# A three-stage kernel whose first batch of attention is done in two passes, with the first feed-forward in groups of 320 and 256 tokens

## Chip, cores and metric

One core of a Trainium2 chip runs the whole program. The metric is the device time of one execution in microseconds, the median of the runs, lower is better.

## The reference

Three stages follow one another, all in float32 (the weights come as float64 and are split by the kernel):

```python
# q, k, v: (4 batches, 8 heads, 576 tokens, 64)
scores = scale * np.matmul(q, k.transpose(0, 1, 3, 2))
mask = pos[:, None] // 64 >= pos[None, :] // 64        # blocks of 64 tokens, causal
attn = softmax(np.where(mask, scores, -1e9))
x = np.matmul(attn, v)                                 # to (2304 tokens, 512)
h = x @ moe_w_in                                       # 512 x 2048
x = np.maximum(0.01 * h, h) @ moe_w_out                # 2048 x 512
h = x @ moe2_w_in
P = a[0] + a[1] * h + a[2] * h**2 + a[3] * h**3
Q = 1.0 + abs(b[0]) * abs(h) + abs(b[1]) * h**2
out = (P / (Q + 1e-6)) @ moe2_w_out
```

## The kernel before

**Split products.** For accuracy most operands are split into a high and a low part (fp32r), and a product is summed from three matmuls: high by high, high by low, low by high. The first batch's attention is plain fp32, whose matmuls appear as two instructions each.

**Attention.** The 32 heads (4 batches of 8) are walked one after another in the loop over `heads`. A head has 576 queries in five tiles of 128 with `KEYS` = 64, 192, 320, 448 and 576 keys (`FIRST` gives each tile's first query). Each letter of the order string is one step of head n: `1` splits q and k of head n+1 (`a1`) and issues loads of q and k; `v` splits v (`a1v`) and, for odd heads, issues the load of a later pair's v (`load_v`); `x`, `y`, `z` compute scores of tile 4, tiles 3 and 2, tiles 1 and 0 (`a2_part`: matmuls L291 or L297, row maxima on VectorE L303, exponentials on ScalarE L309), after the last of them `a2_norm` (L315, L316, and five multiplications on GpSimd, L319); `a` and `b` transpose the probabilities of head n-1 on TensorE (L346) and copy them from PSUM (`evacuate`, L329 to L339); `4` multiplies those of head n-2 by the values (`a4`, L374, L378) and writes the result into the token tiles `X[b]` (L391 to L398). In the first batch (`n < NSF`, `WHOLE`), q is scaled on ScalarE by L245 and `pTw`, a view of `acc`, holds the transposed probabilities.

**First feed-forward.** `moe1(b)` is a generator over one batch of 576 tokens. It has 32 units: 16 of `in` (128 hidden columns each) and 16 of `out` (4 groups times 4 column tiles of the result). A unit is 12 products in two halves of 288 columns, so 24 matmuls (L455), summed in one PSUM tile and then read by ScalarE and VectorE (L468 to L477). `fill(n)` issues the next n matmuls; after each step of a head the numbers of `FILL` or `FILL1` are issued (93 a head). The feed-forward of a batch is queued when the last head of the batch has been applied; so none runs during the first batch's attention, and the fourth batch's runs after the attention. The high weights of it stay in SBUF (`w1i`, `w1o`); the low weights are loaded from DRAM (`W1L`) by `prep_w1`, two units ahead, into three buffers (L429).

**Conversion.** The float64 weights are read as pairs of integers in 64 blocks of 512 KB (`load_block`, L148), three staging buffers `cs`. `convert()` is a generator with two half-steps a block. ScalarE (L168; GpSimd for the first 16 blocks, L166) scales the high word, ScalarE the low word (L172); VectorE puts the sign into the low word (L179) and joins both words (L181); ScalarE rounds to the high part (L184), GpSimd subtracts to the low part (L185); SP writes the parts to DRAM (L156). `pace` issues half-steps so that by the end of head n there are `due[n]` of them; `prep_w1` forces more if a unit needs them (`cv_to`, by groups of four blocks, `NEED`). Blocks of 128 rows by 512 columns are converted group by group.

**Second feed-forward.** From about 683 us `moe2` streams all tokens in chunks of 512 through the second pair of weights (L558, L612).

**Queues and PSUM.** SP's order of DMA issues is the program's; the other engines' order is a scheduler's that follows the program's order closely. All tiles of PSUM in the attention and the first feed-forward share one pool of four (`psA`, 1024 columns each).

```python
due = [0, 2, 4, 5, 9, 11, 13, 17, 22, 29, 36, 42, 48, 59, 65] + [65 + 63 * n // 17 for n in range(1, 18)]
ORDER = "4vx1yabz"
ORDER0 = "1xy4azbv"
ORDERS = "1yzx4vab"
FILL = (12, 1, 0, 8, 18, 9, 13, 32)
ORDER1 = "14vxyabz"
FILL1 = (0, 10, 5, 7, 18, 10, 7, 36)
```

## Time and profile before

| | us |
|---|---|
| median of three runs | 1080.43 |
| the three runs | 1082.78, 1080.43, 1076.47 |
| profiled execution, its time | 1077.4 |
| its span, first to last instruction | 1075.6 |
| TensorE matmul busy | 1015.4 (94%) |
| VectorE busy | 770.2 (72%) |
| ScalarE busy | 661.4 (61%) |
| GpSimd busy | 314.2 (29%) |
| mean granted TensorE clock | 0.986 |

Busy time is the time in which an engine executes at least one instruction; matmuls are pipelined and their ends are modelled, so a busy TensorE isn't one at its peak. The page's second part gives the same in 40 slices of 26.9 us: TensorE's row is `6878888898999999999999999899999999999998`, in tenths. PE is TensorE's matmuls, PEld its weight loads, DVE VectorE, ACT ScalarE, POOL GpSimd, SP the queue that issues DMAs. Names such as L455 are lines of the kernel before.

### The profile page before, as it was taken

To read this page: it belongs to the slowest core of one execution; us is meant where nothing else is said; L and a number is where in the kernel's file an instruction comes from. 1 tells how busy PE (TensorE), PEld (TensorE's weight loads), DVE (VectorE), ACT (ScalarE), POOL (GpSimd) and SP (SyncE) were. 2 spreads that over 40 slices of the span, in tenths; PEclk is the share of its full clock that TensorE was granted. 3 is DMA by queue.
4 is the path that set the end of the run, shared out by engine and by line. 5 is a ranking of instruction groups with operands and counts; after the bars stand their busy time and mean duration, and the time that the engine had idled before them with its cause. 6 is when DMAs were issued, how large, how long until landed. Compare 5 with 4: busy or idle time off the path is not lost.

```text
span 1075.6 us, 16845 instructions
## 1 busy us (share of the span) xinstructions
PE 1015.4 (94%) x6120; PEld 911.1 (85%) x6120; DVE 770.2 (72%) x1261; ACT 661.4 (61%) x1319; POOL 314.2 (29%) x368
## 2 busy tenths in 40 slices
PE   6878888898999999999999999899999999999998
PEld 4557888898989999999999999788888888888887
DVE  3778778886767775877632222698988888888876
ACT  5766656855756665666632111777776676676675
POOL 5687545555444555545320001100000000000000
PEclk9999899999999999999999999999999999999999
DMA  7458566856766567665445845812000110110010
GB/s 190 135 150 252 155 192 189 261 169 203 218 190 175 185 201 237 200 196 168 145 132 197 329 127 171 340 56 79 4 36 9 70 40 1 40 40 1 1 40 20
DMA packets 99954, 149.01 MB, mean 139 GB/s; under 512 B 8224, under 2 KB 52256, under 8 KB 99872
## 3 DMA queue, kind: packets, MB, share of 16 engines
q1 hardware_dynamic: 99872, 147.95, 43.7%
q8 instruction: 48, 0.79, 0.3%
q14 instruction: 34, 0.28, 0.1%
HBM read 108.01 MB, written 39.32 MB: 137 GB/s over the span
## 4 chain that ended last, share of the span: by engine, by line
PE 53%; issue 11%; DMA 8%; DVE 6%; ACT 3%; POOL 2%; SPq 1%; POOLq 0%; ACTq 0%; DVEq 0%
PE o L612 18%; PE h L558 18%; PE M L455 12%; DMA cs<-in_moe_w_in_dram 4%; DMA cs<-in_moe_w_out_dram 3%; PE T L297 2%; PE T L346 2%; PE T L378 1%; POOL acc L482 1%; DVE cl L181 1%; ACT cs L168 1%; ACT cs L172 1%; DVE cs L179 1%; DVE pTl L339 1%; DVE nm L303 1%
## 5 line engine op out<-in xcount | busy, mean ns | idle before, releaser
L319 POOL TENSOR_SCALAR PB<-PB,sm 128x448 f32<-128x448 f32 (+4 forms) x160 | 104.7, 674 | 58.0 <-DVE sm L316 49.5
L309 ACT ACTIVATE PB<-T,nm 128x448 f32<-128x448 f32 (+4 forms) x160 | 83.1, 524 | 55.8 <-DVE nm L303 52.0
L455 PE MATMUL M<-gh,wl 128*128 128x288 f32 x512 | 114.0, 299 | 1.1 <-DMA wl<-w1l 1.1
L455 PE MATMUL M<-gh,w1o 128*128 128x288 f32 x512 | 113.8, 300 | 1.3 <-DVE pTl L339 0.6
L455 PE MATMUL M<-gl,w1o 128*128 128x288 f32 x512 | 111.6, 298 | 1.0 <-DVE gl L470 1.0
L570 ACT ACTIVATE ea<-h,coef 128x512 f32<-128x512 f32 (+1 forms) x80 | 51.7, 647 | 92.7 <-PE h L558 88.9
L470 DVE TENSOR_TENSOR gl<-M,gh 128x576 fp32r<-128x576 f32 x64 | 47.8, 749 | 65.7 <-ACT M L469 65.6
L558 PE MATMUL h<-x2h,w2h 128*128 128x512 f32 (+1 forms) x240 | 89.6, 373 | 4.1 <-DVE eu L581 3.2
L455 PE MATMUL M<-xh,w1i 128*128 128x288 f32 x512 | 84.6, 299 | 8.5 <-DVE pTl L339 3.8
L179 DVE SCALAR_TENSOR_TENSOR cs<-cs 128x512 int32<-128x512 int32 x64 | 60.1, 938 | 44.7 <-ACT cs L172 33.2
L558 PE MATMUL h<-x2h,w2l 128*128 128x512 f32 (+1 forms) x240 | 89.4, 373 | 0.0
L558 PE MATMUL h<-x2l,w2h 128*128 128x512 f32 (+1 forms) x240 | 89.3, 372 | 0.0
L455 PE MATMUL M<-xl,w1i 128*128 128x288 f32 x512 | 86.0, 301 | 2.2 <-DVE xl L392 1.3
L468 ACT ACTIVATE gh<-M 128x576 fp32r<-128x576 f32 x64 | 41.7, 652 | 75.3 <-PE M L455 75.0
L303 DVE TENSOR_REDUCE nm<-T 128x1 f32<-128x448 f32 (+4 forms) x160 | 71.5, 479 | 21.7 <-PE T L291 13.5
L573 DVE SCALAR_TENSOR_TENSOR ea<-eh,coef,ea 128x512 f32<-128x512 f32 (+1 forms) x80 | 55.9, 699 | 41.4 <-ACT eh L571 40.8
L455 PEld LDWEIGHTS M<-gh,wl 128*128 128x128 f32 x512 | 83.6, 190 | 1.6 <-DMA wl<-w1l 1.6
L455 PEld LDWEIGHTS M<-gh,w1o 128*128 128x128 f32 x512 | 83.0, 190 | 2.2 <-ACT w1i L184 0.8
L612 PE MATMUL o<-w2h,g2l 128*128 128x512 f32 x216 | 84.9, 393 | 0.0
L612 PE MATMUL o<-w2h,g2h 128*128 128x512 f32 x216 | 84.8, 393 | 0.0
L612 PE MATMUL o<-w2l,g2h 128*128 128x512 f32 x216 | 84.6, 392 | 0.0
L455 PEld LDWEIGHTS M<-gl,w1o 128*128 128x128 f32 x512 | 83.1, 190 | 1.3 <-DVE gl L470 1.3
(113 smaller groups left out, 2614.9 us busy)
## 6 DMA issues: line engine op xcount, KB each, us to landing
wl<-w1l SPq DMA_DIRECT2D x128, 256.0 KB, 3.0
cs<-in_moe_w_in_dram SPq DMA_DIRECT2D x32, 512.0 KB, 5.3
cs<-in_moe_w_out_dram SPq DMA_DIRECT2D x32, 512.0 KB, 4.6
w1l<-cl SPq DMA_DIRECT2D x32, 256.0 KB, 5.0
w2h<-ch SPq DMA_DIRECT2D x32, 256.0 KB, 4.9
w2l<-cl SPq DMA_DIRECT2D x32, 256.0 KB, 5.1
w2h<-w2h SPq DMA_DIRECT2D x12, 512.0 KB, 7.4
w2l<-w2l SPq DMA_DIRECT2D x12, 512.0 KB, 8.1
```

Of the source, the lines that this page charges most:

```text
L179: nc.vector.scalar_tensor_tensor(lo, hi, -(2 ** 31), lo, ALU.bitwise_and, ALU.bitwise_or)
L297: nc.tensor.matmul(T[:, po:po + w], lhsT=lhs[e][:, FIRST[i]:FIRST[i] + P], rhs=rhs[e][:, c:c + w], start=(lhs is QT), stop=(lhs is QM),)
L303: nc.vector.tensor_reduce(nm[:, i:i + 1], sc, axis=AX.X, op=ALU.max, negate=True)
L309: nc.scalar.activation(PB[e][i][:, 0:ln], sc, AF.Exp, scale=SCALE if n == 0 else 1.0, bias=nm[:, i:i + 1], accum_out=sm[:, i:i + 1])
L319: nc.gpsimd.tensor_scalar(PB[e][i][:, 0:ln], PB[e][i][:, 0:ln], sm[:, i:i + 1], 1.0, ALU.mult, ALU.mult)
L455: nc.tensor.matmul(T[:, e * 512:e * 512 + NH2], lhsT=w[:, kk, :], rhs=a[:, e * NH2:(e + 1) * NH2], start=(n == 0), stop=(n == 11),)
L468: nc.scalar.activation(gh2, res, AF.Prelu, alpha=0.01)
L470: nc.vector.tensor_tensor(gl2, res, gh2.bitcast(F32), ALU.subtract)
L558: nc.tensor.matmul(h[:, 0:n], lhsT=a, rhs=x, start=(kk == 0 and i == 0), stop=(kk == KD - 1 and i == 2))
L570: nc.scalar.activation(a, h, AF.Abs, scale=coef[:, 4:5])
L573: nc.vector.scalar_tensor_tensor(a, h2, coef[:, 5:6], a, ALU.mult, ALU.add)
L612: nc.tensor.matmul(ob[t], lhsT=a, rhs=w, start=(f == 0 and i == 0), stop=(f == NF - 1 and i == 2))
```

## The change

The first batch's attention is walked twice over its 8 heads. Pass A (items 0 to 7) computes query tiles 0, 1 and 2, that is tokens 0 to 319, which need keys 0 to 319 alone; pass B (items 8 to 15) computes tiles 3 and 4, tokens 320 to 575. Then come the 24 heads of the other batches (items 16 to 39). The first feed-forward of the first batch is done in two groups, of 320 and 256 tokens, each with all 32 units of 12 matmuls without halves; the first is queued after pass A and filled into pass B, 4 matmuls after each of five steps. Batch 1's heads have 76 fills in place of 93. q is no more scaled; the factor is in the exponential, and each part scales its row maxima and has its own reciprocal. The two transposed-probability tiles alternate.

Conversion blocks are now one unit's weights each (four row tiles by 128 columns), in the order in which units need them. ScalarE does all high-word scalings, by a Prelu whose slope for negative values puts the sign where the join needs it; L179 and the GpSimd scalings are gone. The low part of a first-matrix block is written by GpSimd into one of eight places in the token tiles of batch 1, over the oldest that no unit is using, besides its write to DRAM; a unit of the first group whose block is still there uses it, and otherwise loads it from DRAM as before. The places close with item 16.

```diff
-    pTh = ap.tile([P, 1664], F32R, name="pTh")
-    pTl = ap.tile([P, 1664], F32R, name="pTl")
+    pTw = [ap.tile([P, 1664], F32, tag=f"pt{i}", name=f"pTw{i}") for i in range(2)]
...
+    CUTS = [5, 9, 13, 16]
     blocks = []
-    for wi, wo, which in ((w1_in, w1_out, 1), (w2_in, w2_out, 2)):
-        for g in (0, 1, 4, 2, 5, 3, 6, 7) if which == 1 else (0, 4, 1, 5, 2, 6, 3, 7):
-            for r in range(4):
-                if g < 4:
-                    src = wi[r * P:(r + 1) * P, 2 * g * 512:2 * (g + 1) * 512]
-                    fs = slice(4 * g, 4 * g + 4)
-                    if which == 1:
-                        dst = w1i[:, r, g * 512:(g + 1) * 512], W1L[fs, :, r, :]
-                    else:
-                        dst = W2H[fs, :, r, :], W2L[fs, :, r, :]
-                else:
-                    f = 4 * (g - 4) + r
-                    src = wo[f * P:(f + 1) * P, :]
-                    if which == 1:
-                        dst = w1o[:, f, :], W1L[NF + 4 * (g - 4):NF + 4 * (g - 3), :, r, :]
-                    else:
-                        dst = tuple(W[f:f + 1, :, KD:2 * KD, :] for W in (W2H, W2L))
-                blocks.append((src, dst, which == 1))
+    for g, c in enumerate(CUTS):
+        for f in range(CUTS[g - 1] if g else 0, c):
+            src = w1_in[:, 2 * f * P:2 * (f + 1) * P].rearrange("(r p) w -> p r w", p=P)
+            blocks.append((src, (w1i[:, :, f * P:(f + 1) * P], W1L[f]), True))
+        for d in range(KD):
+            src = w1_out[512 * g:512 * (g + 1), 2 * d * P:2 * (d + 1) * P].rearrange("(r p) w -> p r w", p=P)
+            blocks.append((src, (w1o[:, 4 * g:4 * g + 4, d * P:(d + 1) * P], W1L[NF + 4 * g + d]), True))
+    for f in range(NF):
+        src = w2_in[:, 2 * f * P:2 * (f + 1) * P].rearrange("(r p) w -> p r w", p=P)
+        blocks.append((src, (W2H[f, :, 0:KD, :], W2L[f, :, 0:KD, :]), False))
+        src = w2_out[f * P:(f + 1) * P, :].rearrange("p (r w) -> p r w", r=KD)
+        blocks.append((src, (W2H[f, :, KD:2 * KD, :], W2L[f, :, KD:2 * KD, :]), False))
...
+    live, pinned, places, closed = {}, set(), [], []
...
-                if i in NPG:
-                    nc.gpsimd.tensor_scalar(hi.bitcast(F32), hi.bitcast(F32), 2.0 ** -112, 1.0, ALU.mult, ALU.mult)
-                else:
-                    nc.scalar.activation(hi.bitcast(F32), hi.bitcast(F32), AF.Copy, scale=2.0 ** -112)
-                if i in NPC:
-                    nc.gpsimd.tensor_scalar(lo, lo.bitcast(U32), 0.875 * 2.0 ** -29, 0.4375, ALU.mult, ALU.add)
-                else:
-                    nc.scalar.activation(lo, lo.bitcast(U32), AF.Copy, scale=0.875 * 2.0 ** -29, bias=0.4375)
+                nc.scalar.activation(
+                    hi.bitcast(F32), hi.bitcast(F32), AF.Prelu, scale=2.0 ** -112, alpha=-(2.0 ** 32)
+                )
+                nc.scalar.activation(lo, lo.bitcast(U32), AF.Copy, scale=0.875 * 2.0 ** -29, bias=0.4375)
...
-                f = cp.tile([P, 512], F32, tag="cl", name="cl", bufs=3)
-                wh = dh if kept else cp.tile([P, 512], F32R, tag="ch", name="ch", bufs=2)
-                nc.vector.scalar_tensor_tensor(lo, hi, -(2 ** 31), lo, ALU.bitwise_and, ALU.bitwise_or)
+                f = cp.tile([P, KD, P], F32, tag="cl", name="cl", bufs=3)
+                wl = f.bitcast(F32R)
+                if kept and not closed:
+                    p = min((p for p in range(len(places)) if live.get(p) not in pinned), key=lambda p: live.get(p, -1))
+                    live[p] = i - 1
+                    wl = places[p]
...
-                nc.gpsimd.tensor_tensor(f.bitcast(F32R), f, wh.bitcast(F32), ALU.subtract)
+                nc.gpsimd.tensor_tensor(wl, f, wh.bitcast(F32), ALU.subtract)
...
+    CUT = 320
+    items = [("A", n) for n in range(H)] + [("B", n) for n in range(H)] + [("S", n) for n in range(H, NHD)]
+    NW = 2 * H
...
+        if v < NW:
+            dq, dk = (T[0:D, :] for T in plain[v % 4])
+            cq_, ck = (slice(0, CUT), slice(0, CUT)) if kind == "A" else (slice(CUT, S), slice(0, S))
+            nc.sync.dma_start(out=dk[:, ck], in_=k[b, h][:, ck])
+            nc.sync.dma_start(out=dq[:, cq_], in_=q[b, h][:, cq_])
+            return
...
+    def load_v(vp):
+        if 2 * vp >= len(items):
+            return
+        kind, n = items[2 * vp]
+        b, j = divmod(n // 2, NP)
+        s, dst = v[b, j], vr[vp % 2 if 2 * vp < NW else 0]
+        nt = 3 if kind == "A" else 4
+        nc.sync.dma_start(out=dst[:, 0:nt, :], in_=s[0:nt * P].rearrange("(t p) c -> p t c", p=P))
...
+    def a2_norm(e, sm, tiles):
+        c = slice(min(tiles), max(tiles) + 1)
+        nc.vector.tensor_scalar(sm[:, c], sm[:, c], 1e-9, None, ALU.add)
+        nc.vector.reciprocal(sm[:, c], sm[:, c])
...
+    def w2_part(v, tiles, st):
+        nm, sm = st
+        fq, fk = plain[v % 4]
+        T = psA.tile([P, 1024], F32, tag="A", name="T")
+        done = []
+        for o, i in tiles:
+            ln = KEYS[i]
+            parts = [(o, 0, max(ln, P))] if i < 4 else [(512 - NH2, 0, NH2), (512, NH2, NH2)]
+            for po, c, w in parts:
+                nc.tensor.matmul(
+                    T[:, po:po + w], lhsT=fq[:, FIRST[i]:FIRST[i] + P], rhs=fk[:, c:c + w], start=True, stop=True
+                )
+            done.append((i, ln, T[:, parts[0][0]:parts[0][0] + ln]))
+        softmax(v % 2, done, nm, sm, SCALE)
+        a2_norm(v % 2, sm, [i for _, i in tiles])
...
+    def w3(v, part):
+        e, pw = v % 2, pTw[v % 2]
+        if items[v][0] == "A":
+            if part == 0:
+                T = psA.tile([P, 1024], F32, tag="A", name="T")
+                for kt, o in ((0, 0), (1, 576), (2, 832)):
+                    for i in range(kt, 3):
+                        c = o + FIRST[i] - START[kt]
+                        nc.tensor.transpose(T[:, c:c + P], PB[e][i][:, kt * P:(kt + 1) * P], ident)
+                nc.scalar.copy(pw[:, 0:CUT], T[:, 0:CUT])
+                nc.vector.tensor_copy(pw[:, 320:640], T[:, 576:896])
+        elif part == 0:
+            T = psA.tile([P, 1024], F32, tag="A", name="T")
+            for kt in range(4):
+                for i in (3, 4):
+                    c = 256 * kt + P * (i - 3)
+                    nc.tensor.transpose(T[:, c:c + P], PB[e][i][:, kt * P:(kt + 1) * P], ident)
+            nc.scalar.copy(pw[:, 0:512], T[:, 0:512])
+            nc.vector.tensor_copy(pw[:, 512:1024], T[:, 512:1024])
+        else:
+            T = psA.tile([P, 1024], F32, tag="A", name="T")
+            nc.tensor.transpose(T[:, 0:P], PB[e][4][:, 4 * P:5 * P], ident)
+            nc.vector.tensor_copy(pw[:, 1024:1024 + P], T[:, 0:P])
+    def w4(v):
+        kind, n = items[v]
+        e, j = n % 2, n // 2
+        pw, vv = pTw[v % 2], vr[(v // 2) % 2]
+        T = psA.tile([P, 1024], F32, tag="A", name="T")
+        if kind == "A":
+            c, w = 0, CUT
+            parts = ((0, 0, 320, 0), (1, 128, 192, 320), (2, 256, 64, 576))
+        else:
+            c, w = CUT, S - CUT
+            parts = tuple((kt, 0, 256, 256 * kt) for kt in range(4)) + ((4, 128, 128, 1024),)
+        for kt, o, m, s0 in parts:
+            nc.tensor.matmul(
+                T[:, o:o + m], lhsT=vv[:, kt, :], rhs=pw[:, s0:s0 + m], start=(kt == 0), stop=(kt == parts[-1][0])
+            )
+        r = slice(e * 64, e * 64 + 64)
+        xh, xl = X[0]
+        nc.scalar.copy(xh[r, j, c:c + w], T[r, 0:w])
+        nc.vector.tensor_tensor(xl[r, j, c:c + w], T[r, 0:w], xh[r, j, c:c + w].bitcast(F32), ALU.subtract)
...
+    groups = [(0, 0, CUT), (0, CUT, S - CUT)] + [(b, 0, S) for b in range(1, B)]
+    NU = 2 * NF
...
-                cv_to(NEED["in", i // 4] if kind == "in" else NEED["out", i])
+                cv_to(w + 1)
...
+            held = [p for p in live if live[p] == w]
+            if held:
+                wl = places[held[0]]
+                pinned.add(w)
+            else:
+                wl = mp.tile([P, 4, P], F32R, tag="wl", name="wl", bufs=3)
+                nc.sync.dma_start(out=wl.bitcast(F32), in_=src)
...
+    def moe1(g):
+        b, t0, n = groups[g]
         xh, xl = X[b]
-        base = b * (len(units) // B)
-        for u in range(base, base + len(units) // B):
+        half = [(0, 0, NH2), (512, NH2, NH2)] if n > 512 else [(0, 0, n)]
...
+                for o, c, nn in half:
                     nc.tensor.matmul(
-                        T[:, e * 512:e * 512 + NH2], lhsT=w[:, kk, :],
-                        rhs=a[:, e * NH2:(e + 1) * NH2],
-                        start=(n == 0), stop=(n == 11),
+                        T[:, o:o + nn], lhsT=w[:, kk, :], rhs=a[:, c:c + nn], start=(m == 0), stop=(m == 11)
...
+        due = [1, 2, 3, 5, 7, 9, 11, 13, 17, 21, 25, 28, 31, 34, 37, 40, 48, 57, 65]
+        due += [65 + 63 * n // 21 for n in range(1, 22)]
...
+        PLAN = {
+            "A": ("x4a", (0, 0, 0)),
+            "B": ("x4ayb", (4, 4, 4, 4, 4)),
+            "S0": ("14vxyabz", (0, 8, 4, 6, 15, 8, 6, 29)),
+            "S1": ("14vxyabz", (0, 10, 5, 7, 18, 10, 7, 36)),
+            "S": ("4vx1yabz", (12, 1, 0, 8, 18, 9, 13, 32)),
+        }
...
+                if kind == "S":
+                    a4(n)
+                else:
+                    w4(t)
+                    if t % 2 and t + 3 <= NW:
+                        load_v(t // 2 + 2)
+                if n % H == H - 1:
+                    if kind == "S":
+                        drain()
+                    queue.append(moe1(t // H if t < NW else n // H + 1))
...
+                for x in X[1]:
+                    x = x.rearrange("p k s -> p (k s)")
+                    places.extend(x[:, 512 * c:512 * (c + 1)].rearrange("p (r c) -> p r c", c=P) for c in range(4))
+            if t == NW:
+                closed.append(True)
+            if t == NW + 2:
+                assert not pinned & set(live.values())
+                live.clear()
```

## Rows read from the trace of the kernel before

**Rows 1.** Windows by stage: length; busy (count) PE, PEld, DVE, ACT, POOL; PEclk, DMA, GB/s.

```profile
0.00:12.00 12.00, 7.31 (x20) 4.67 (x20) 3.35 (x10) 6.05 (x15) 5.24 (x24) 1.00 0.77 175
12.00:92.00 80.00, 65.69 (x317) 47.66 (x318) 57.85 (x111) 52.35 (x129) 59.28 (x75) 0.94 0.54 162
92.00:261.00 169.00, 150.91 (x1067) 145.40 (x1065) 132.86 (x205) 113.15 (x239) 96.64 (x106) 0.96 0.66 200
261.00:417.00 156.00, 147.38 (x1079) 143.27 (x1078) 113.95 (x186) 100.95 (x217) 81.52 (x89) 0.99 0.65 200
417.00:551.00 134.00, 128.38 (x951) 124.82 (x951) 90.52 (x154) 83.46 (x181) 58.61 (x68) 1.00 0.60 179
```

**Rows 2.** Groups by line: shapes, count, busy us, mean ns, idle before, its releasers.

```profile
L179 DVE SCALAR_TENSOR_TENSOR cs<-cs 128x512 int32<-128x512 int32 x64 | 60.1, 938 | 44.7 <-ACT cs L172 33.2 <-POOL cs L166 11.2
...
L181 DVE SCALAR_TENSOR_TENSOR cl<-cs 128x512 int32<-128x512 int32 x64 | 57.7, 903 | 1.1
...
L172 ACT ACTIVATE cs<-cs 128x512 int32<-128x512 uint32 x64 | 43.3, 676 | 2.1 <-DMA cs<-in_moe_w_in_dram 1.0 <-DMA cs<-in_moe_w_out_dram 1.0
...
L168 ACT ACTIVATE cs<-cs 128x512 f32<-128x512 f32 x48 | 32.6, 680 | 42.5 <-DMA cs<-in_moe_w_in_dram 24.3 <-DMA cs<-in_moe_w_out_dram 18.1
...
L166 POOL TENSOR_SCALAR cs<-cs 128x512 f32<-128x512 f32 x16 | 13.7, 858 | 5.3 <-DMA cs<-in_moe_w_in_dram 5.2
...
L184 ACT CAST w1i<-cl 128x512 fp32r<-128x512 f32 x16 | 9.9, 619 | 9.1 <-DVE cl L181 9.0
...
L315 DVE TENSOR_SCALAR sm<-sm 128x5 f32<-128x5 f32 x32 | 8.5, 264 | 2.2 <-ACT PB L309 1.8
...
L316 DVE RECIPROCAL sm<-sm 128x5 f32<-128x5 f32 x32 | 5.9, 185 | 0.5
```

**Rows 3.** Waits of PE from 0 to 245 us: total, times, longest.

```profile
PE T L297 <- DVE vr L395: 8.8, 4, 4.0
PE T L346 <- POOL PB L319: 7.1, 10, 4.1
```

**Rows 4.** A window of L455 alone: length, PE busy (count), PEld busy (count).

```profile
572.00:620.00 48.00, 48.00 (x365) 48.00 (x365) 1.00 0.72 260
```

**Rows 5.** Timeline of PE near 1007 us: start us, us, instruction.

```profile
1004.78 0.39 PE L558 MATMUL h<-x2h,w2h 128*128 128x512 f32 x1
...
1007.50 0.39 PE L612 MATMUL o<-w2h,g2h 128*128 128x512 f32 x1
...
1010.23 0.28 PE L558 MATMUL h<-x2h,w2h 128*128 128x256 f32 x1
...
1011.55 0.28 PE L558 MATMUL h<-x2h,w2l 128*128 128x256 f32 x1
```

**Rows 6.** Timeline of PE in the first batch's attention.

```profile
49.82 2.75 PE L378 MATMUL T<-acc,vr 128*128 128x448 f32 x10
```

**Rows 7.** Waits of ACT from 261 to 551 us.

```profile
ACT cs L168 <- DMA cs<-in_moe_w_in_dram: 19.7, 10, 4.0
...
ACT cs L168 <- DMA cs<-in_moe_w_out_dram: 12.1, 7, 3.4
```

**Rows 8.** Instructions of L179 and L429: ns min/median/max, first and last start us.

```profile
L179 DVE SCALAR_TENSOR_TENSOR cs<-cs x64: 652/695/2249, 21.4 to 523.5; 128x512 int32<-128x512 int32 x64
...
L429 SPq DMA_DIRECT2D wl<-w1l x128: 319/320/1490, 92.7 to 661.3; - x128
```

**Rows 9.** Waits of SP's queue, whole run.

```profile
SPq L429 <- PE M L455: 244.3, 89, 7.2
...
SPq L239 <- PE T L378: 17.0, 3, 8.5
```

**Rows 10.** DMA issues: count, KB each, median us to landing.

```profile
wl<-w1l SPq DMA_DIRECT2D x128, 256.0 KB, 3.0
cs<-in_moe_w_in_dram SPq DMA_DIRECT2D x32, 512.0 KB, 5.3
...
w1l<-cl SPq DMA_DIRECT2D x32, 256.0 KB, 5.0
```

More of the change, by code (lines that the diff above doesn't have):

```diff
@@ L147, in load_block @@
             stage[i] = cp.tile([P, 512, 2], I32, tag="cs", name="cs", bufs=3)
-            nc.sync.dma_start(out=stage[i].rearrange("p n w -> p (n w)"), in_=blocks[i][0])
+            nc.sync.dma_start(out=stage[i].rearrange("p (r n) w -> p r (n w)", r=KD), in_=blocks[i][0])
     split = []
@@ L324, in attention_moe_moe_kernel, with evacuate @@
     OFF = [0, 896, 1344, 576, 768]
     START = [0, 128, 256, 384, 448]
-    def evacuate(T, s0, n, d0, whole, on_vector):
-        if whole:
-            (nc.vector.tensor_copy if on_vector else nc.scalar.copy)(pTw[:, d0:d0 + n], T[:, s0:s0 + n])
-            return
+    def evacuate(T, s0, n, d0):
+        if not pT:
+            pT.extend(ap.tile([P, 1664], F32R, tag=f"pt{i}", name=f"pT{i}") for i in range(2))
+        pTh, pTl = pT
         nc.scalar.copy(pTh[:, d0:d0 + n], T[:, s0:s0 + n])
@@ new lines, in attention_moe_moe_kernel @@
+        for t, (kind, n) in enumerate(items):
+            odd, h = n % 2, n % H
+            if h == 0 and kind != "B" and n != H:
+                X[n // H] = x_tiles()
+            if t == 0:
+                X[1] = x_tiles()
+                for x in X[1]:
[6 more added lines that the diff above has]
+                live.clear()
@@ L695, in attention_moe_moe_kernel @@
             nm = mp.tile([P, 5], F32, tag="nm", name="nm")
             sm = mp.tile([P, 5], F32, tag="sm", name="sm")
-            steps, fills = (
-                (ORDERS, FILL) if n == 0 else (ORDER0, FILL) if n < 9 else (ORDER1, FILL1) if n < 17 else (ORDER, FILL)
-            )
-            for step, f in zip(steps, fills):
-                if step == "1" and n + 1 < NHD:
+            steps, fills = PLAN[kind if kind != "S" else "S0" if n < 16 else "S1" if n < 17 else "S"]
+            for s, (step, f) in enumerate(zip(steps, fills)):
+                if step == "1" and t + 1 < len(items):
@@ L722, in attention_moe_moe_kernel @@
[L722 to L729 removed]
+                    a2_norm(n % 2, sm, [3, 4, 0, 1, 2])
+                fill(f)
+                pace(t, (s + 1) * 8 // len(steps))
+            if t + 4 < NW:
+                load_qk(t + 4)
+            if t == NW - 3:
+                load_qk(NW)
```

229 lines of the change are left out of this document (91 added, 138 removed).

## The prediction

> **What bounds the kernel now.** I read the busy time by stage first, then the costliest groups, the waits of TensorE and of SP's queue, and last single matmuls in the timeline. The stages [rows 1] show TensorE near its bound from 92 us on: busy 150.9 of 169, 147.4 of 156 and 128.4 of 134 us while three batches of attention are interleaved with the first feed-forward. In the first batch's attention, 0 to 92, it is busy 73.0 (7.31 and 65.69) and idle 19.0. Idle time is 18.1 from 92 to 261, and 8.6 and 5.6 after it. The granted clock is 0.94 from 12 to 92, which is some 12% of that stretch at 1.2 GHz and the rest at 2.4 GHz. Those idle microseconds, 51.3 before 551, are all that this change can win; the matmuls stay. VectorE (132.9 of 169) and ScalarE (113.2 of 169) are the next busiest, and much of their work is the conversion of the weights [rows 2]. What TensorE waits for are GpSimd's normalization (7.1 us) and VectorE's read of a PSUM tile, L395 (8.8 us) [rows 3].
>
> The sum runs against the profiled execution, 1077.4 us (span 1075.6 and 1.8 around it). The median of the three runs is 3.0 higher; differences are added to the median, 1080.4.
>
> **The change, part by part.**
>
> *Columns.* A matmul of 288 columns takes 131.5 ns in a dense stretch (365 in 48.0 us), of 512 columns 227 ns (2.72 us over 12), of 256 columns 120 ns (1.32 us over 11 steps) [rows 4, 5]. Between 288 and 512 a line gives 145 ns for 320. So 384 pairs of 320 and 256 cost 384 x (145 + 120 - 263) = +0.8 us. The values product of the first batch streams 1728 columns a head instead of 1664; at 2.75 us for 1536 columns [rows 6] that is 8 x 0.115 = +0.9 us. Scores and transposes keep their number (15 transposes a head).
>
> *What moves.* Seven of the eight items of pass B have 20 fills: 140 of the 384 matmuls of the first group, 140 x 0.145 = 20.3 us of TensorE, now lie before the attention of batch 1. Batch 1's eight heads then have 76 fills each in place of 93, and the ninth item 20. At the start of head 17 both versions have issued the matmuls of one whole batch, so that point, now at 261 us, is where I compare.
>
> *Stage one, now 92 us.* TensorE work becomes 73.0 + 20.3 + 0.9 = 94.2. Idle now 19.0. The fills can sit in the gaps between scores and transposes of pass B, but pass A has short items (3 of 5 score tiles, 6 of 15 transposes) and the same chain of reduce, exponential, reciprocal and normalization behind each. Bounds: 8 (pass B without a gap; less is excluded by the 4.6 us before the first score and the filling of the chain) and 30 (ScalarE sets the pace). I take 15, nearest to the present 19 less a few that fills cover: 109, or **+17**. The extra small operations are 16 pairs of L315 and L316 (0.264 + 0.185, 7.2 us of VectorE) [rows 2]; with 24 short scalings of the row maxima they lie beside TensorE's work, and without that cover they are inside the upper bound.
>
> *The conversion comes earlier.* The list of due times asks for 20 blocks by the end of pass B, against 8.5 by the end of head 7 now. ScalarE's part of a block is 0.680 + 0.676 + 0.619 us; for the first 16 blocks GpSimd did the 0.680 part (13.7 us in all) [rows 2]. So ScalarE gets 20 x 1.975 less 8.5 x 1.295, +28 us on the 58.4 it has, less 7 scalings of q (estimated at 0.68 each): some 82 of 109 before the Prelus of the new fills. VectorE loses L179 everywhere, 60.1 us over 64 blocks, and here pays 20 x 0.903 in place of 8.5 x 1.841, +2.4. In the new loop the hi and lo scalings of ScalarE now directly await the loads.
>
> The rows on that: from 261 to 551 us ScalarE's hi scaling waited 19.7 and 12.1 us for the loads [rows 7], over 26 blocks 1.22 us each; but none of TensorE's leading waits [rows 3] is on that. I price 16 more such waits at 0 in the forecast, bounds 0 and 16 x 1.22 = 19.5. The Trainium skill says in its page Perfetto Trace Analysis, section Tensor Engine Instruction, that ScalarE, VectorE and GpSimd execute strictly first in, first out; by that rule each exponential behind a late load is late too, which is the last rival below, and the sum would be 19.5 higher. The trace does not contradict the rule, it only shows little of it reaching TensorE.
>
> *Stage two, now 169 us (92 to 261).* TensorE: 150.9 - 140 x 0.1315 + 244 x 0.0135 - 384 x 0.0115 = 150.9 - 18.4 + 3.3 - 4.4 = 131.4. Idle now 18.1. Less: VectorE's L179 goes, and with it the place where VectorE stands behind ScalarE's scaling before it reads the PSUM tile that TensorE wants (8.8 us [rows 3]); I take 7 of it. More: items 17 and 18 convert about 9.5 blocks and load 13 lo weights, 0.786 MB a block and 0.262 MB a load, some 6 MB an item with q, k and v. This stage moves 200 GB/s now at a share of 0.66 of the DMA engines [rows 1], which at full share is 303: 20 us an item, where TensorE needs 17 to 18. Bounds for the two items: 0, if loads issued ahead carry them, and 24, if they move at today's 200; I take 5, nearest to the full share. Idle 16: 147.4, or **-21.6**. Bounds of idle here: 8 and 30.
>
> *Stage three, 261 to 551.* Idle is 14.2. By head 17, 85 half-steps of conversion are done against 72, so 6 blocks fewer remain of 28, and each is 0.94 us of VectorE cheaper. Bounds 0 and -10; I take **-6**. From 551 on nothing changes.
>
> *Lo weights from SBUF and the queue.* Following fills, due times and the eight places in order, 13 of the first group's 32 units find their block in SBUF; the other 19 were overwritten or came after the places closed. With five groups instead of four, loads are 160 - 13 = 147 against 128. SP also issues 16 more loads of q and k and 4 more of v: 39 issues at some 0.32 us [rows 8], 12 us of SP over 550, off the path. Each v load of the passes follows the last product that reads its buffer, and SP stands there (17.0 us in three waits now [rows 9]) with the loads of conversion blocks behind it, so ScalarE's wait for a block is what comes late next; its bound is in the 19.5 above. Blocks of W1 are loaded in pieces of 1 KB in place of 4 KB and written in pieces of 2 KB in place of 512 B; a block lands in 5.3 us and a write in 5.0 now [rows 10], and I price this at 0, bounds 2 either way.
>
> Sum: +17 - 21.6 - 6 = -10.6, from 1080.4 to **1070 us**. The forecast's own range is 1064 to 1076.
>
> **The rivals.**
>
> *More relief, 1056 us.* VectorE's L179 takes 652 ns at least and 938 on the mean, up to 2249 [rows 2, 8]: 64 x 0.286 = 18.3 us are time in which it stands, not works. If those stops and GpSimd's own end with it, TensorE's idle time falls to 8 in stage two and by 10 in stage three: 1070 - 8 - 4, and 2 from stage one, 1056. The Trainium skill, page SBUF — State Buffer, section Who interferes with whom, gives such a stop a cause: VectorE and GpSimd share a port pair as an exclusive lock. The spread of L179 agrees with it, though no row names the lock. Against: VectorE has slack in every stage.
>
> *One for one, 1080 us.* The moved matmuls find no gaps: idle stays 19 in pass A and B plus what pass A's short chain adds (22), stage two keeps 18, stage three gains 5. The sum is +24.2 - 19.5 - 5 = 0. For: the total of TensorE's work is the same; against: 19 idle microseconds stand in stage one.
>
> *Lo weights late, 1090 us.* A unit of the first two groups has 12 matmuls, not 24. Three buffers let a load be issued two units before its use; that was 2 x 3.16 us and is 2 x 1.6 to 1.7 in the long runs of fills. A load lands in 3.0 us (median) after an issue of 0.32 [rows 8, 10], and SP already spends 244 us waiting for these buffers [rows 9]. Units 20 to 63, 44 of them, depend on it. If landing, with the other traffic, rises to the 4.2 us that lies between 3.0 and the 5.3 of a block, each lacks 0.9 us in dense runs, half of the units: 20 us, in batch 1's attention. It decides from landing plus issue above 3.3 us.
>
> *ScalarE held by loads, 1089 us.* The 19.5 us above, all of it in items 0 to 18, reaching TensorE.
>
> **How the numbers follow.** A measurement of this kernel tells some 0.5%, 5.4 us, from no change: faster is below 1075, slower above 1086. Forecast 0.36 (0.30 of it faster, 0.06 same), more relief 0.22, one for one 0.20, lo weights late 0.12, ScalarE held 0.10. That makes faster 0.52, same 0.26, slower 0.22. The range, 1055 to 1088, takes in the relief and the one-for-one case and leaves out the two slow ones, whose upper parts are above it.
>
> **What would show it.** Pass A over near 42 us and pass B near 109; head 17 starting near 256; idle of TensorE about 15 and 16 in the two stages; VectorE some 45 us less busy in all and ScalarE some 10 more. Waits of TensorE on wl above 10 us would mean the lo-weight rival, waits of ScalarE for cs blocks before 130 us with TensorE idle beside them the last one. If pass B alone takes over 80 us, the step on stage one is wrong; if head 17 starts after 265, the forecast is.

## The result, and the profile after

The changed kernel took 1090.87 us (median of 5 runs, 1087.81 to 1093.82), the kernel before 1080.43 beside it (1075.65 to 1082.78): 1.011 times as long, 95% interval 1.008 to 1.014. It is slower by some 10 us. Forecast was 1070, with a range of 1055 to 1088.

The busy times of the profile's page; against before (the last line of each windows view below), TensorE is busy 6.3 us longer and idle 4.2 us longer, VectorE 43 less, ScalarE 9 more:

```profile
span 1086.1 us, 17083 instructions
...
PE 1021.7 (94%) x6152; PEld 919.0 (85%) x6152; DVE 727.2 (67%) x1298; ACT 670.3 (62%) x1380; POOL 290.5 (27%) x356
```

To compare versions I cut each at its own events: the moment at which VectorE takes the reciprocal of head 8 (batch 1's first), of head 16 and of head 31. "Head 16 comes at" means this moment. The kernel before, so cut (columns as in [rows 1]):

```profile
0.00:90.00 90.00, 71.00 (x324) 50.57 (x325) 59.26 (x119) 57.76 (x141) 62.53 (x98) 0.94 0.58 167
90.00:255.70 165.70, 147.61 (x1041) 141.92 (x1040) 132.51 (x202) 110.91 (x235) 93.72 (x100) 0.96 0.65 197
255.70:541.10 285.40, 271.15 (x1994) 263.99 (x1994) 202.03 (x335) 182.60 (x394) 142.47 (x157) 0.99 0.64 194
541.10:1075.60 534.50, 525.61 (x2766) 454.57 (x2764) 376.37 (x607) 310.13 (x550) 15.46 (x14) 1.00 0.25 86
sum 1075.60, PE 1015.38 PEld 911.05 DVE 770.17 ACT 661.41 POOL 314.19; mean PE 253.84 PEld 227.76 DVE 192.54 ACT 165.35 POOL 78.55
```

The changed kernel: pass A, pass B, up to head 8, up to head 16, up to head 31, the rest; then its second stage as the prediction cut it:

```profile
0.00:51.00 51.00, 31.54 (x133) 23.96 (x134) 24.34 (x72) 28.48 (x85) 22.36 (x53) 0.87 0.62 166
51.00:117.00 66.00, 62.73 (x353) 52.51 (x354) 45.55 (x119) 50.67 (x110) 39.31 (x42) 1.00 0.84 257
117.00:129.40 12.40, 11.59 (x80) 11.11 (x80) 7.92 (x17) 10.42 (x25) 5.73 (x5) 1.00 0.90 274
129.40:282.40 153.00, 126.76 (x872) 117.28 (x870) 98.33 (x185) 99.61 (x239) 82.86 (x95) 0.97 0.71 219
282.40:553.10 270.70, 263.97 (x1959) 259.55 (x1958) 174.90 (x302) 171.37 (x375) 124.79 (x149) 0.99 0.57 176
553.10:1086.10 533.00, 525.11 (x2766) 454.55 (x2764) 376.21 (x606) 309.71 (x550) 15.45 (x14) 1.00 0.24 85
...
117.00:285.00 168.00, 140.06 (x956) 129.64 (x955) 108.36 (x205) 111.14 (x265) 90.85 (x102) 0.97 0.71 220
```

Head 16 comes at 282.4 in place of 255.7, 26.7 us late. Of that 14.7 come back up to head 31 and 1.5 after it. Pass A has TensorE idle for 19.5 of 51 us, pass B for 3.3 of 66. From head 8 to head 16 only 872 matmuls are issued, 169 fewer than before, in 153.0 us instead of 165.7: TensorE has 20.9 us less to do there (126.8 for 147.6), most of it moved forward into pass B, and the stretch became 12.7 us shorter. The waits of TensorE from 0 to 285 us (total, times, longest):

```profile
PE M L510 <- DMA wl<-w1l: 8.2, 9, 2.1
PE T L374 <- ACT pTw L347: 7.9, 3, 3.8
PE T L405 <- ACT PB L307: 7.2, 4, 2.5
PE T L346 <- POOL PB L317: 4.4, 3, 2.8
```

No single one explains 27 us. ScalarE's wait for block loads is there too, from 51 to 285 us:

```profile
ACT cs L158 <- DMA cs<-in_moe_w_in_dram: 12.3, 10, 2.1
ACT cs L158 <- DMA cs<-in_moe_w_out_dram: 8.1, 7, 1.9
```

### The profile page after: what moved, and what is told of

The parts are those of the page before. It is cut to its first block, busy times and chain, and to the rows that moved or that the text cites. A ratio compares the mean times of both kernels' runs of the same rounds, so it can differ in the third digit from the quotient of the medians.

```text
span 1086.1 us, 17083 instructions
## 1 busy us (share of the span) xinstructions
PE 1021.7 (94%) x6152; PEld 919.0 (85%) x6152; DVE 727.2 (67%) x1298; ACT 670.3 (62%) x1380; POOL 290.5 (27%) x356
## 4 chain that ended last, share of the span: by engine, by line
PE 53%; issue 16%; DMA 12%; DVE 6%; ACT 6%; POOL 5%; SPq 3%; POOLq 0%; DVEq 0%; ACTq 0%
PE o L669 18%; PE h L615 18%; PE M L510 11%; DMA cs<-in_moe_w_in_dram 5%; DMA cs<-in_moe_w_out_dram 3%; PE T L437 2%; POOL PB L317 2%; PE T L405 2%; DMA wl<-w1l 2%; PE T L292 1%; POOL acc L540 1%; POOL cl L179 1%; DMA w2l<-cl 1%; ACT PB L307 1%; ACT cs L158 1%
## 5 line engine op out<-in xcount | busy, mean ns | idle before, releaser
L510 PE MATMUL M<-gh,w1o 128*128 128x288 f32 (+2 forms) x512 | 124.9, 303 | 5.1 <-DVE gl L528 1.7
L510 PE MATMUL M<-gh,wl 128*128 128x288 f32 (+2 forms) x488 | 118.3, 302 | 5.2 <-DMA wl<-w1l 5.2
L510 PE MATMUL M<-gl,w1o 128*128 128x288 f32 (+2 forms) x512 | 122.2, 300 | 0.6 <-DVE gl L528 0.6
L307 ACT ACTIVATE PB<-T,nm 128x320 f32<-128x320 f32 (+4 forms) x160 | 83.0, 523 | 50.7 <-DVE nm L301 35.0
L317 POOL TENSOR_SCALAR PB<-PB,sm 128x320 f32<-128x320 f32 (+4 forms) x160 | 93.8, 604 | 63.1 <-DVE sm L314 47.7
L528 DVE TENSOR_TENSOR gl<-M,gh 128x576 fp32r<-128x576 f32 (+2 forms) x80 | 50.6, 633 | 74.0 <-ACT M L527 73.4
L510 PE MATMUL M<-xh,w1i 128*128 128x288 f32 (+2 forms) x512 | 87.9, 303 | 4.4 <-ACT xh L446 1.4
L510 PE MATMUL M<-xl,w1i 128*128 128x288 f32 (+2 forms) x512 | 87.7, 300 | 0.0
L175 DVE SCALAR_TENSOR_TENSOR cl<-cs 128x512 int32<-128x512 int32 x64 | 54.0, 845 | 50.1 <-ACT cs L161 27.7
L301 DVE TENSOR_REDUCE nm<-T 128x1 f32<-128x320 f32 (+4 forms) x160 | 72.2, 482 | 22.9 <-PE T L331 11.5
```

The costliest lines, as they stand in the source:

```text
L175: nc.vector.scalar_tensor_tensor(f.bitcast(I32), hi, 3, lo, ALU.logical_shift_left, ALU.bitwise_or)
L301: nc.vector.tensor_reduce(nm[:, i:i + 1], sc, axis=AX.X, op=ALU.max, negate=True)
L307: nc.scalar.activation(PB[e][i][:, 0:ln], sc, AF.Exp, scale=scale, bias=nm[:, i:i + 1], accum_out=sm[:, i:i + 1])
L317: nc.gpsimd.tensor_scalar(PB[e][i][:, 0:ln], PB[e][i][:, 0:ln], sm[:, i:i + 1], 1.0, ALU.mult, ALU.mult)
L510: nc.tensor.matmul(T[:, o:o + nn], lhsT=w[:, kk, :], rhs=a[:, c:c + nn], start=(m == 0), stop=(m == 11))
L528: nc.vector.tensor_tensor(as_psum(gl), res, as_psum(gh).bitcast(F32), ALU.subtract)
```

## The experiments

Ratios are to the kernel before on the same chip in the same session; differences in us are differences of ratios times 1080.4. In the cuts of code `nc.` is left out, and `...` stands for what is left out.

**1 and 2. The sign alone, and the change without it.** The kernel before with only the sign placement; and the changed kernel with VectorE's operation and GpSimd's 16 scalings back.

```diff
-if i in NPG: gpsimd.tensor_scalar(hi, hi, 2.0 ** -112, ...)
-else: scalar.activation(hi, hi, AF.Copy, scale=2.0 ** -112)
+scalar.activation(hi, hi, AF.Prelu, scale=2.0 ** -112, alpha=-(2.0 ** 32))
...
-vector.scalar_tensor_tensor(lo, hi, -(2 ** 31), lo, bitwise_and, bitwise_or)
```

> The sign part alone in the kernel before: Prelu on ScalarE, no L179, no scaling on GpSimd. Theory (late conversion loads hold the passes and the first heads of batch 1; the sign part is a gain): 1068 to 1073, head 17 no later than before and the later heads some 8 us shorter. Rival (the later heads got shorter in the changed kernel because six blocks fewer were left for them, not by the sign): 1078 to 1083.

> The changed kernel with the old sign operation on VectorE and the first 16 high-word scalings on GpSimd. Theory: 8 to 12 us above the changed kernel, 1099 to 1103, the difference in the heads after batch 1. Rival (ScalarE's added scalings are what slows pass A): pass A ends 5 us or more earlier and the time is within 5 us of the changed kernel or below it.

The sign alone: 1054.45, ratio 0.977 (0.9745 to 0.9795), -25 us, faster than both kernels and beyond every forecast. Without it the change takes 1104.72, ratio 1.0232 (1.0202 to 1.0262): the sign is worth 13 there, 12 of them before head 8 (141.5 for 129.4) and not behind batch 1 as expected. So the rest of the change costs 36 us against sign alone. The windows of sign alone, cut at the same events:

```profile
0.00:82.00 82.00, 70.18 (x331) 50.82 (x332) 49.91 (x108) 64.23 (x155) 52.51 (x87) 0.98 0.66 183
82.00:235.50 153.50, 141.10 (x1036) 135.87 (x1035) 108.57 (x177) 112.64 (x238) 84.59 (x94) 1.00 0.70 212
235.50:515.80 280.30, 269.14 (x1995) 262.28 (x1994) 178.43 (x308) 183.13 (x394) 136.71 (x157) 1.00 0.65 197
515.80:1050.50 534.70, 526.28 (x2766) 455.25 (x2764) 376.22 (x606) 310.46 (x550) 15.38 (x14) 0.99 0.25 86
sum 1050.50, PE 1006.71 PEld 904.22 DVE 713.12 ACT 670.46 POOL 289.18; mean PE 251.68 PEld 226.06 DVE 178.28 ACT 167.62 POOL 72.30
```

It gains 8 us to head 8, 12 from there to head 16 and 5 from there to head 31. TensorE's idle time falls from 60.2 to 43.8, and its busy time by 8.7 with the same matmuls: 1036 of them took 141.1 us at a granted clock of 1.00, 1041 had taken 147.6 at 0.96. Of the idle time from head 8 to head 16, 5 us are TensorE's wait for VectorE's read of a PSUM tile (L395 [rows 3], L393 in this version), 3.8 in place of 8.8:

```profile
PE T L295 <- DVE vr L393: 3.8, 4, 1.4
```

**3. GpSimd's share of it.** The kernel before, with ScalarE scaling the first 16 blocks (`NPG = range(0)`).

> The kernel before with one edit: the hi scaling of the first 16 blocks on ScalarE instead of GpSimd, the sign still placed by VectorE. It splits the 25 us that the sign placement alone gained. Theory: the gain is VectorE's (64 operations off its queue), so GpSimd's 16 scalings are worth little here and ScalarE's 16 more cost little: 1074 to 1082. Rival: GpSimd's softmax scalings were behind its block scalings, and their going is half of the gain: 1064 to 1070.

1076.16, ratio 0.9953 (0.9939 to 0.9968): 5 of the 25 us are GpSimd's relief. The other 20 came with the end of VectorE's operation.

**4. The block shape.** Sign alone, plus blocks of one unit each in unit order.

```diff
-src = wi[r * P:(r + 1) * P, 2 * g * 512:2 * (g + 1) * 512]
+src = w1_in[:, 2 * f * P:2 * (f + 1) * P].rearrange("(r p) w -> p r w", p=P)
```

> The kernel with the sign placement alone (1054 us) plus one part: the conversion blocks in the order and shape of the feed-forward's units (loads in pieces of 1 KB for the first weights, forced conversion a block at a time). Theory: the loads move the same bytes and lie ahead of their use, so 1052 to 1060. Rival: the small pieces land later and ScalarE stands for them, in strict order, in every head: 1066 to 1075.

1063.05, ratio 0.983 (0.9809 to 0.9852): it costs 6.5 us by the ratios. The loads land as before (a block in 4.8 and 5.4 us, 4.9 and 4.9 in sign alone), so what in the new shape, order or block-by-block forcing costs was not settled.

**5. The passes alone.** The changed kernel with the first batch's feed-forward whole, behind both passes.

```diff
-groups = [(0, 0, CUT), (0, CUT, S - CUT)] + [(b, 0, S) for b in range(1, B)]
+groups = [(b, 0, S) for b in range(B)]
-due = [1, 2, 3, 5, 7, 9, 11, 13, 17, 21, 25, 28, 31, 34, 37, 40, 48, 57, 65] + ...
+due = [0, 1, 2, 3, 4, 5, 6, 7, 8, 9, 10, 11, 12, 13, 15, 17, 22, 29, 36, 42, 48, 59, 65] + ...
-"S0": ("14vxyabz", (0, 8, 4, 6, 15, 8, 6, 29)),
+"S0": ("14vxyabz", (0, 10, 5, 7, 18, 10, 7, 36)),
-places.extend(...)   # so no lo block is held
```

> The changed kernel with the passes kept and the rest taken back: the first batch's feed-forward is one group of 576 tokens after both passes, no lo block stays in SBUF, the conversion goes at the pace of the kernel before. Theory: the passes themselves lose about 20 us against 1054 (sixteen short items whose chain of scores, softmax, copy and product ends on other engines, with TensorE at a lower clock): 1070 to 1080. Rival: the passes are cheap and the loss comes from mixing them with feed-forward fills and front-loaded conversion: 1055 to 1063.

1076.69, ratio 0.9952 (0.9932 to 0.9973), 13 us above experiment 4's version. Its windows (pass A, pass B, head 8, head 16):

```profile
0.00:44.00 44.00, 28.68 (x134) 22.48 (x135) 22.62 (x70) 25.71 (x79) 21.18 (x53) 0.92 0.58 161
44.00:94.00 50.00, 41.00 (x203) 31.34 (x203) 34.08 (x98) 30.30 (x68) 25.42 (x31) 0.97 0.51 147
94.00:100.60 6.60, 5.65 (x29) 4.86 (x28) 5.99 (x11) 4.65 (x15) 3.23 (x4) 0.74 0.99 320
100.60:259.30 158.70, 144.82 (x1038) 139.61 (x1037) 110.71 (x177) 114.33 (x242) 83.12 (x94) 0.98 0.65 205
```

Head 8 comes at 100.6; in experiment 4's version it came at 83.6, and from there on both take the same (to head 16 158.7 and 159.1 us, to head 31 281.1 and 281.6). The cost is in the passes. Pass A takes 44 us here with 7 half-blocks of conversion, 51 in the changed kernel with 13.

**6. The groups without the early start.** The changed kernel with no fills in pass B, and 93 fills a head behind it. A held block that is still to be used keeps its place beyond item 18, since the first group now comes later.

```diff
-"B": ("x4ayb", (4, 4, 4, 4, 4)),
+"B": ("x4ayb", (0, 0, 0, 0, 0)),
-"S0": ("14vxyabz", (0, 8, 4, 6, 15, 8, 6, 29)),
+"S0": ("14vxyabz", (0, 10, 5, 7, 18, 10, 7, 36)),
...
-live.clear()
+for p in [p for p in live if live[p] not in pinned]: live.pop(p)
```

> The changed kernel without feed-forward work in its second pass (160 matmuls, 21 us of TensorE, go back behind it, at the fill of the kernel before). Theory: the early start of the feed-forward buys next to nothing, since heads 8 to 16 take their 153 us with 164 matmuls fewer as well: 1084 to 1094. Rival: the second pass hides those 21 us and they come back on the path: 1100 to 1112.

1103.09, ratio 1.0193 (1.0151 to 1.0235). The theory that the early start buys next to nothing fell: it is worth 9 us (12 by the medians) of the 21 moved. But this version is 26 us above the passes alone: so much do the groups, with their held blocks and early conversion, cost. The early start has to pay for that:

```profile
0.00:51.00 51.00, 31.16 (x133) 23.60 (x134) 24.75 (x72) 28.47 (x85) 22.36 (x53) 0.87 0.61 167
51.00:104.00 53.00, 41.92 (x213) 31.67 (x212) 38.18 (x101) 41.34 (x89) 34.81 (x38) 1.00 0.91 280
104.00:125.60 21.60, 15.19 (x82) 13.82 (x82) 14.14 (x25) 16.21 (x38) 10.93 (x12) 0.84 0.70 224
125.60:294.00 168.40, 145.74 (x1009) 138.17 (x1007) 103.04 (x198) 102.41 (x245) 75.28 (x93) 0.96 0.66 208
```

Against the passes alone: +7 in pass A, +3 in pass B, +15 up to head 8 (with 53 matmuls more by then), +10 from there to head 16, and -8 up to head 31. With the fills, pass B is 66 us instead of 53 for 140 matmuls more: 8 of their 21 us are hidden there.

**7. The groups without passes.** Sign alone, with (a) both groups one after the other behind all eight heads; (b) the two sizes within each unit, weights converted and read once, at the old pace; (c) as (a), but a unit whose block is not yet converted does not wait: it multiplies by the latest converted one of its kind.

```diff
-filler[0] = moe1(b)
+queue.extend(moe1(g) for g in ((0, 1) if b == 0 else (b + 1,)))   # (a)
+for t0, n in ((0, 320), (320, 256)) if b == 0 else ((0, S),):     # (b)
+while NEED[kind, i // 4 if kind == "in" else i] > ndone[0]: i -= 1 # (c)
```

> The kernel with the sign placement alone took 1054 us; this adds one part to it, the first batch's feed-forward as a group of 320 and a group of 256 tokens, both after all eight heads, with every lo block read from DRAM (160 reads for 128). Theory: what the changed kernel loses against 1054 (36 us) comes from the two passes and from what is squeezed into them, and the short units cost little: 768 matmuls at 0.147 and 0.120 us between starts against 0.132 is +1 us, and 64 more evacuations cost some idle: 1055 to 1064. Rival: the short units, which turn the matmul buffers over every 1.7 us instead of 3.2, are what slows heads 8 to 16 (about 20 us lost there): 1072 to 1078.

> The kernel with the sign placement alone (1054 us), with each unit of the first batch's feed-forward worked as 320 and then 256 tokens in two matmul buffers, evacuated apart; the unit's weights are converted and read once, at the old pace. Two groups one after the other took 1104. Theory: of those 50 us nearly all came from needing every converted block in the time of the first group, half the time that the kernel before has, so short units alone give 1054 to 1064. Rival: the short units and their doubled evacuations are the cost: 1080 to 1104.

> The kernel with the sign placement and the two groups of tokens one after the other (1104 us), where no unit waits for its own block: a unit whose block is not yet converted takes the latest converted block of its kind, so the conversion keeps the pace of the kernel before (the first batch's feed-forward is then left with wrong weights). Theory: the 40 us between 1104 and the 1064 of short units alone come from forcing all 32 blocks through in the first group's time: 1062 to 1075. Rival: they come from the 32 more reads of lo blocks or from the order of the units, and stay: 1092 to 1106.

(a) 1104.07, ratio 1.0215 (1.0194 to 1.0237), +48 us over sign alone. (b) 1064.44, ratio 0.9854 (0.9828 to 0.988), +9. (c) 1081.5, ratio 1.0011 (0.9981 to 1.0041). So short units cost 9, forcing all 32 blocks through in half the time 22, and 17 are left for the order of the units and the 32 more reads of lo blocks, which were not taken apart. From head 8 to 16 in (a), (b) and (c):

```profile
81.70:290.20 208.50, 161.11 (x1022) 149.69 (x1020) 124.38 (x217) 134.66 (x306) 103.98 (x107) 0.89 0.79 252
```

```profile
82.50:242.90 160.40, 143.32 (x1034) 137.43 (x1033) 111.38 (x207) 115.38 (x272) 86.23 (x96) 0.99 0.68 206
```

```profile
82.80:262.70 179.90, 152.63 (x1028) 143.36 (x1026) 110.19 (x208) 119.85 (x279) 88.43 (x99) 0.94 0.78 242
```

TensorE's idle time is 47, 17 and 27 us, and nearly the same matmuls take 161, 143 and 153 us at a granted clock of 0.89, 0.99 and 0.94: the version with more idle time has the longer busy time too.

**8. Which wait.** The changed kernel with (a) each v load of the passes one item later, (b) no reads of lo blocks for the two groups (an earlier block is used), (c) no engine waiting for block loads (they still move their bytes, but the conversion works on the first block's data again and again), (d) both (b) and (c), (e) a fourth load buffer, with one buffer less each for the converted block and its copy.

```diff
-load_v(t // 2 + 2)
+later.append((min(cur[0] + 1, NW - 1), t // 2 + 2))                  # (a)
+elif ub < 2 and w > 0: wl = last[0]                                   # (b)
+t = one[0] if i == 0 else cp.tile([P, 512, 2], I32, tag="cs", bufs=2) # (c)
+stage[i] = one[0]                                                     # (c)
-load_block(i + 1)
+load_block(i + 2)                                                     # (e)
```

> The changed kernel with each load of v in the passes issued one item later, so that the queue does not stand at it with conversion loads behind it. Theory (a ring: v load waits for the product, the conversion load behind it lands 5.6 us later, ScalarE waits for it and holds the copy that the next product needs): pass A ends near 43 us in place of 50 and the time is 6 to 8 us below the changed kernel, 1083 to 1085. Rival (the short items' own chain of reduce, exponential and normalization sets pass A): pass A within 2 us, the time unchanged, 1089 to 1093.

> Left out: the loads of lo weights for the first batch's two groups; those units multiply by one that is there already. Theory (in items 17 to 19 the lo load waits for its own write, with conversion loads behind it): items 17 to 20 lose 10 to 15 us of their 86, the rest of batch 1's heads little; 1075 to 1081. Rival one (units of 12 matmuls are too short for three buffers everywhere): items 21 to 24 gain as much as items 17 to 20, 1065 to 1075 in all. Rival two (ScalarE is the bound there): at most 4 us.

> The changed kernel where every block's load is still issued and moves its bytes, but into buffers that nobody reads: the conversion works over and over on the first block's data, so no engine waits for a load after the first (the weights of the feed-forwards are left wrong). Theory: the waits for loads are most of what the front-loaded conversion costs: 1066 to 1077. Rival: the time goes to the conversion's operations themselves, or to the shared traffic of the queues: 1084 to 1092.

> The changed kernel with both loads taken off the path at once: no lo block of the first batch's groups is read back (an earlier one is used) and no engine waits for a block's load after the first (the loads still move their bytes); the weights are wrong. Each alone gave -3 and +2 us. Theory: each wait hid the other in heads 9 to 12, and without both 10 to 18 us go: 1073 to 1081. Rival: neither is what sets those heads' time, and their own chain through ScalarE and VectorE does: 1084 to 1092.

> The changed kernel with four buffers for a block's load instead of three, so each load goes out one block earlier (and one buffer less each for the converted block and its copy, to make room). Theory: ScalarE, which takes its instructions strictly in order, stands in front of block loads that have not landed, and all that is behind it waits: a load more in flight gives back a part, 1074 to 1084. Rival: the loads are there in time for what counts, and the conversion's own work in the way is the cost: 1086 to 1096.

(a) 1093.34, ratio 1.0136 (1.0095 to 1.0178); (b) 1087.7, 1.0074 (1.0048 to 1.0101); (c) 1093.32, 1.0128 (1.0094 to 1.0162); (e) 1090.35, 1.0081 (1.0051 to 1.011): all within 4 us of the change, their intervals over its own. (d) 1080.58, ratio 1.0006 (0.9972 to 1.0039): 11 us less. TensorE's costliest wait up to 285 us was, with the lo reads gone, one for a matmul buffer that ScalarE's exponential gives back; with the load waits gone, from 51 us on, it was the lo reads:

```profile
PE M L513 <- ACT PB L307: 11.6, 5, 3.7
```

```profile
PE M L514 <- DMA wl<-w1l: 10.7, 8, 2.6
```

So each wait stood behind the other, and only both together give time back. (d)'s ten runs go from 1076.4 to 1090.5 and its profile is of the slowest of them, so no line of it is shown. Even there head 16 comes at 272.0 in place of 282.4; by head 31 that run has lost it again (552.9 and 553.1).

**9. The conversion's pace.** (a) The changed kernel with 3.7 half-blocks an item from head 8 on, nothing forced (as in 7c, a unit takes a converted block in place of a late one); (b) sign alone with a more even list, (c) sign alone with the fourth load buffer, (d) sign alone with q scaled by GpSimd.

> The changed kernel with the conversion spread evenly from head 8 on (3.7 half-blocks an item, not 8, 9 and 8 in the first three) and nothing forced: a unit whose block is not yet converted takes the latest converted one of its kind (wrong weights). Theory: the 13 blocks pressed into items 16 to 18 are what holds heads 9 to 11 up by some 15 us, since the time there is the conversion's and not TensorE's: 1070 to 1080. Rival: those items are held by their own chain of softmax and copies whatever the conversion does: 1086 to 1094.

> The kernel with the sign placement alone (1054 us) with its conversion spread more evenly: 23 half-blocks by head 7 for 17, and no head with more than 8, where one had 11. Theory: where the conversion sets the time of heads 9 to 14, taking 6 half-blocks out of them gives 3 to 8 us: 1046 to 1052. Rival: heads 0 to 7 lose as much as heads 9 to 14 gain: 1052 to 1060.

> The same edit of the load buffers on the kernel with the sign placement alone (1054 us). Theory: ScalarE waits some 15 us for block loads in heads 8 to 16 there too, a part of it on the path: 1046 to 1052. Rival: no gain, or a loss from the buffers given up: 1053 to 1060.

> The kernel with the sign placement alone (1054 us), with the scaling of the first batch's q moved from ScalarE, which stands 5.6 us for the q loads there, to GpSimd, which no longer scales blocks. Theory: a few us of the first 72 go: 1049 to 1053. Rival: GpSimd's softmax scalings, on which TensorE waits 4.2 us there, come later by as much: 1054 to 1060.

(a) 1091.54, ratio 1.0089 (1.0055 to 1.0122): no change in all. Head 11 came 8.5 us sooner (189.3 for 197.8) and head 31 4.3 later: what was not converted early is paid later. (b) 1054.66, ratio 0.9745 (0.9713 to 0.9777), and (d) 1055.48, 0.9762 (0.9734 to 0.979): the same as sign alone. (c) 1061.14, 0.9821 (0.9781 to 0.9861): not faster, and slower by some 5 us as far as intervals that just touch can tell. None is faster than sign alone by more than the noise.

## Why the prediction was wrong

Chained by ratios: sign -25, block shape +6.5, passes +13, groups with held blocks and early conversion +26, early start in pass B -9. These steps add up to the changed kernel's own ratio (+12, 10 by the medians) by the way they are taken, so the sum is no check on them, and each holds for the parts that were in place when it was added. The prediction's -10.6 had a sign for each stage, and the steps fared like this.

- **Stage one, +17: measured +25** (117 for 92). The step that failed is idle 15: it was 22.7, and 19.5 of it in pass A. Pass B was 66 us as forecast (67), pass A 51 for 42. Seven of the nine came with the early conversion and its held blocks, for which the sum has nothing: with the old pace pass A took 44. Most of the seven are ScalarE's waits for block loads. Without these waits (8c) the 133 matmuls that the changed kernel has issued by 51 us are there at 45:

```profile
0.00:45.00 45.00, 28.96 (x133) 23.39 (x134) 20.96 (x69) 28.86 (x85) 23.61 (x54) 0.89 0.74 198
```

TensorE's work came out to a tenth (94.2 forecast; 31.5 + 62.7), in part by luck: of what the sum had put there, 12 score matmuls of batch 1 and 9 transposes of head 7 come behind 117 us, and 7 more fills and products in more pieces (118 matmuls for 96) stand in their place.

- **Stage two, -21.6: measured -1** (168.0 in the row 117 to 285, for 169; up to head 16's reciprocal, +2). This is the step that turned the sign, and head 17 starts near 285, not 256. Taken were 131.4 of work and 16 of idle; the row shows 140.1 and 27.9. The idle term had 5 us for the traffic of two items and nothing for the two waits that the rivals three and four are about, for lo blocks and for block loads. I held each of these to be worth 20 or nothing; alone each is worth 4 or less, together 11, nearly the 11.9 that the idle term lacks. Of the 8.7 of work some 4 are 29 matmuls more than the 927 that I counted, since the cut at 117 leaves 19 matmuls of head 7 and most of head 8's scores to stage two; the other 5 are a mean of 0.1465 us instead of 0.1417, which I can't assign.
- **The slow rivals' numbers,** 1090 and 1089, lie beside the measured 1090.9 by luck: each has one wait alone as the cause. TensorE's wait for lo blocks, 8.2 us, also stayed under the 10 that was to be rival three's sign.
- **Stage three, -6: measured -14.7** to head 31 (270.7 for 285.4). The direction is right and the size is not. Little of it is VectorE's relief: with the sign operation back (2) the stretch takes 273.0. More is conversion that had been done before it: spread evenly (9a), it takes 278.9:

```profile
297.30:570.30 273.00, 264.39 (x1954) 258.80 (x1955) 191.06 (x321) 170.94 (x373) 126.37 (x149) 0.99 0.57 174
```

```profile
278.50:557.40 278.90, 266.40 (x1957) 260.10 (x1956) 177.25 (x307) 180.06 (x392) 133.06 (x155) 0.99 0.61 188
```

- **The sign, 7 us in stage two and a part of the 6:** alone it is 25. I credited only TensorE's waits on L395 [rows 3], took VectorE's 44.7 us of standing before L179 [rows 2] for slack, and held TensorE's busy time fixed ("the matmuls stay"), of which 8.7 us went as the clock rose. Rival one named the cause and had the size (1056); it lost because the rest of the change cost 36. It rests on the time in which L179 stands, and the lock that it cites for this from the Trainium skill (SBUF — State Buffer, Who interferes with whom) agrees with the trace: of the 64 operations in the kernel before, the 15 with no GpSimd instruction beside them took 0.68 to 0.70 us, and all 27 that took longer, up to 2.25, ran beside one, by the profile's times. One of each, and GpSimd's subtraction beside the second:

```profile
123.64 0.69 DVE L179 SCALAR_TENSOR_TENSOR cs<-cs 128x512 int32<-128x512 int32 x1 [1.09 <-ACT cs L172]
...
138.91 1.78 DVE L179 SCALAR_TENSOR_TENSOR cs<-cs 128x512 int32<-128x512 int32 x1 [1.83 <-ACT cs L172]
```

```profile
138.88 1.26 POOL L185 TENSOR_TENSOR cl<-cl,w1o 128x512 fp32r<-128x512 f32 x1
```

How much of the 20 us these stops are was not measured. Experiment 3 took away only GpSimd's 16 scalings, 13.7 of its 314 us, and L179's mean fell from 938 to 880 ns.

- **Blocks in pieces of 1 KB, priced at 0:** 6.5 with the new order, above the bound of 2.
- **The first-in-first-out rule** of the Trainium skill (Perfetto Trace Analysis, Tensor Engine Instruction) would have made the sum 19.5 us higher. Taking the load waits off ScalarE (8c) gave nothing back (2 us more, within the intervals), so that price did not show; no run tests the order itself. Pass A does get shorter without these waits, but the program does not, because other waits are as late.
- **Right:** VectorE -43 (some 45), ScalarE +9 (some 10), 147 lo reads, and nothing from head 31 on (-1.5).
- **One for one**, the second rival, is nearest for the fills: 13 of 21 us came back in pass B at once.

Left open: what in the block shape costs 6.5, and how the 26 us of the groups divide between early conversion, short units and lo reads where the passes are (7 of them lie in pass A).

## What to carry to other kernels

Run the small part of a change alone first: here one operation taken off VectorE, busy for 79% of stage two [rows 1], was worth most of 25 us, and the large rearrangement around it lost more than that (36). Work that is moved forward is only won if the place it goes to is idle and the place it leaves is bound by it; pass B hid 8 of 21 us, and heads 8 to 16, with 20.9 us less for TensorE to do, became 12.7 shorter. Where two waits are equally late, price them together: here, removing either one alone gave 4 us or less, and both 11.
